# Another order of table, transpose and inverse steps for batch 0, the Gelu table ahead of the products, and batch 1 one slot later

## The chip, the cores and the metric

The kernel runs on one core of a Trainium2 chip. Its five engines work side by side, each through its own queue in program order: TensorE (PE in the profile) multiplies into PSUM, ScalarE (ACT) and VectorE (DVE) copy PSUM results to SBUF and compute on them, GpSimd (POOL) does small copies and issues loads, SyncE (SP) issues the other transfers. The metric is the device time of one execution in microseconds. Eight runs of the kernel before gave a median of 774.5 us (774.27 to 774.85).

## The reference

Every batch of `x` (8 x 3008 x 256) is filtered along the sequence in the frequency domain, and the result goes through a two-matrix block with an exact Gelu:

```python
X = np.fft.rfft(x, axis=1)
Y = X * (filt_r + 1j * filt_i)[None]
y = np.fft.irfft(Y, n=x.shape[1], axis=1)
h = y.reshape(B * S, D) @ w_in            # 24064 x 256 @ 256 x 2048
g = 0.5 * h * (1 + erf(h / sqrt(2)))
out = g @ w_out                           # 2048 -> 256
```

## The kernel before

The 3008-point transform is split as 47 x 64, so that each half is a matrix product with a small table of sines. Four tables are made on the chip: T1 for the 47-point half, T2 for the 64-point half with the twiddle factors in it (24 frequencies k, with three column blocks: sine-type rows in block 1, their swapped and signed twin in blocks 2 and 0), T3, which is T2's blocks 1 and 2 transposed, and T4 and T4c, T1 transposed with weights, for the inverse. `table_2_sin(h)` writes block 1 of one half of T2 on ScalarE, `table_2_swap(h)` makes the other blocks by two TensorE matmuls and, for h = 1, four ScalarE copies of 384 columns, `table_3(q)` transposes eight frequencies on TensorE and copies 1024 columns on ScalarE, `table_4` does the same for T4 and T4c.

**Batch 0** has no other work beside it, so it goes through SBUF and TensorE transposes and not through DRAM. Sixteen `c1` steps do the first half of the transform. `c1t(q)` transposes four frequencies (eight 128x128 transposes) and copies them to tile b(q). `c2(p)` does the second half for two frequencies: four matmuls into a two-bank PSUM tile, and one VectorE product of 1024 columns with the filter F, into tile p(p) (the last one, p = 11, in two pieces of 512). `c3(p)` takes products p and p + 1 through the inverse with T3: sixteen matmuls into two banks and two copies into `vt`; the matmuls of p + 1 stand in its second half. The two last products have a `c3` of eight matmuls each. After that come, in a loop of ten, `c3t` (transposes, a VectorE copy) and `c4` (matmuls with T4c, copies into the ring `y_sb`).

The transposes, `c3` and table steps share four PSUM banks (kind `n`) that are used in rotation, `c2` and the warm-up matmuls two tiles of two banks (kind `w`). A step that takes a bank waits until the copy of the tile four (or two) before it is done. The filter's lower half of partitions is copied to the upper half by `dup_filters`, two frequencies at a time: frequencies 0 to 3 on VectorE, the others on POOL, and product p needs the copy with its frequencies 2p and 2p + 1.

There is no scheduler: `manual_schedule` keeps every engine's instructions in the order in which the Python code issues them, and semaphores for the data and for the buffers are put in. So the order of the calls is the order of the work. In the loop `for q in range(7)` (L578) these calls stand.

**The main loop** (L648) runs over (47 + 1) x 16 slots, sixteen for each tile of 512 tokens. Slot s = 16 t + jc does a quarter of the output matmuls of tile t - 1 (`mm2`, L492) and one block of tile t's first matrix (`mm1`, L465) with its Gelu on ScalarE (L468). The transforms of batches 1 to 7 are put into chosen slots ahead of these by `put(slot, ...)`: `s1` (first half, four per batch, with SP writes to a DRAM tile R1), `r1` (four SP reads back), `s2` (twelve, with two ScalarE copies and three VectorE operations each), `s3` (four slots after its `s2`, SP writes to R2 for every two), `r2` (eight SP reads), `s4` (sixteen, into the ring), and `load_next`, POOL's loads of the next batch. For batch 1 the slots are: `s1` at 0, 4, 8, 12, `r1` at 15, `s2` from 25 on in steps of 2.8, `r2` at 61, `s4` from 68 on in steps of 0.72. Batch 1's rows begin in slot 80.

Of the kernel before, what the change touches and what calls it, by code (L numbers as in the profile page):

```python
# [9 lines left out]
AF = mybir.ActivationFunctionType  # L10
ALU = mybir.AluOpType
FP32 = mybir.dt.float32
BF16 = mybir.dt.bfloat16
# [4 lines left out]
NA, NB = 47, 64  # L18
K1 = 24
# [9 lines left out]
class _Mix:  # L29
# [187 lines left out]
        ts(out=self.wtc, in0=self.p, scalar1=4.0, scalar2=1.0, op0=ALU.is_ge, op1=ALU.add)  # L217


    def table_4(self):  # L220
        nc = self.nc
        ps = self.bank("ps_t4", "n")
        rows = ((self.T4, self.T1p, self.wt), (self.T4c, self.T1q, self.wtc))
        o = [ps[0:96, 128 * i:128 * i + 2 * NA] for i in range(2)]
        for i, (t4, t1, wt) in enumerate(rows):
            nc.tensor.matmul(o[i], lhsT=t1.rearrange("p a b c -> p (a b c)"),
                             rhs=self.eye[0:2 * NA, 0:2 * NA], start=True, stop=True)
        for i, (t4, t1, wt) in enumerate(rows):
            self._evac(t4.rearrange("p n h -> p h n"), o[i].rearrange("p (h n) -> p h n", h=2), "act", wt[0:96])

    def table_3(self, q, eng):
        ps = self.bank("ps_t3", "n", BF16)
# [277 lines left out]
@with_exitstack  # L510
def kernel(
    ctx: ExitStack,
    tc: tile.TileContext,
    x: bass.AP,
    filt_r: bass.AP,
    filt_i: bass.AP,
    moe_w_in: bass.AP,
    moe_w_out: bass.AP,
    out: bass.AP,
):  # L520
    m = _Mix(ctx, tc, x, filt_r, filt_i, moe_w_in, moe_w_out, out)
    nc, B, S = tc.nc, m.B, m.S
    NT = B * S // TCH
    ctx.enter_context(tc.manual_schedule())

    g = m.small
    wide = ctx.enter_context(ExitStack())
    m.psum(wide, w=(2, 2), n=(4, 1))
    act = "act"
    m.p = m.iota(g, "p", [128, 1], [[0, 1]], cm=1)  # L530
    m.load_x(0, 0, 1, (0,))
    m.pi = m.iota(g, "pi", [128, 1], [[0, 1]], cm=1, dt=I32)
    m.load_x(0, 0, 1, (1,))
    m.ones = g.tile([128, 512], BF16, name="ones")
    nc.vector.memset(m.ones, 1.0)
    m.warm_up(10)
    m.table_1(g)
    m.weights_4(g)
    m.T1c = g.tile([2 * NA, 96], BF16, name="T1c")
    nc.vector.tensor_copy(out=m.T1c.rearrange("p (k h r) -> p k h r", h=2, r=2),  # L540
                          in_=m.T1.rearrange("p (h r k) -> p k h r", h=2, r=2))
    m.kk = m.iota(g, "kk", [128, K1 // 2], [[1, K1 // 2]])
    m.jj = g.tile([128, NB], FP32, name="jj")
    for sgn, lo in ((1, 0), (-1, 32)):
        nc.gpsimd.iota(m.jj[:, lo:lo + 32], pattern=[[sgn * NA, 32]], base=min(0, sgn * NA),
                       channel_multiplier=0, allow_small_or_imprecise_dtypes=True)
    cols = m.iota(g, "cols", [128, 128], [[1, 128]])
    m.load_x(0, 1, 4)
    m.gen = m.py.tile([128, 3, K1 // 2, NB], FP32, tag="y", name="gen")
    m.table_2(g)  # L550
    m.table_2_angle(0)
    m.unit_matrices(g, cols)
    m.table_2_angle(1)
    for k, n in ((0, 4), (4, 4), (8, 8), (16, 8)):
        m.load_filters(k, n)
    m.dup_filters(nc.gpsimd, 4, 4)
    m.load_w_in()
    m.dup_filters(nc.gpsimd, 8, 8)


    warm = g.tile([128, 1], FP32, name="warm")
    for u in range(16):
        m.c1(u // 2, u % 2, act if u < 4 or u % 2 else False)
        if u == 3:
            m.warm_up(3)
            m.table_2_sin(0)
        if u == 7:
            m.table_2_swap(0)
            m.table_2_minus()
            m.warm_up(3)  # L570
        if u == 11:
            m.warm_up(2)
    m.table_2_sin(1)
    m.warm_up(2)
    m.c1t(0, False)
    m.c1t(1, act)
    m.dup_filters(nc.vector, 0, 4)
    for q in range(7):  # L578
        if q < 6:
            m.c2(2 * q)  # L580
            if q > 0 and q + 2 < 6:
                m.c1t(q + 2, act)
            m.c2(2 * q + 1)
        if q == 0:
            m.table_3(0, act)
            m.table_2_swap(1)
            m.dup_filters(nc.gpsimd, 16, 8)
            m.T1p = g.tile([2 * NA, 2, K1, 2], BF16, name="T1p")
            nc.gpsimd.tensor_copy(out=m.T1p, in_=m.T1.rearrange("p (h r k) -> p h k r", h=2, r=2))
            m.T1q = g.tile([2 * NA, K1, 2, 2], BF16, name="T1q")  # L590
            nc.gpsimd.tensor_copy(out=m.T1q, in_=m.T1.rearrange("p (h r k) -> p k r h", h=2, r=2))
            m.table_1_tiles(g)
            m.load_x(1)
            m.load_w_out(0)
            m.load_w_out(8)
            m.c1t(2, act)
        if 1 <= q < 3:
            m.table_3(q, act)
        if q >= 1:
            if q < 6:  # L600
                m.c3(2 * q - 2)
            else:
                m.table_4()
                m.c3(10, 1)
                m.c3(11, 1)
        if q == 4:

            nc.scalar.activation(out=warm, in_=m.p, func=AF.Gelu)
    wide.close()
    wide = ctx.enter_context(ExitStack())  # L610
    m.psum(wide, v=(5, 1), t=(3, 1))
    for u in range(10):
        if u < 8:
            m.c3t(u)
        if u >= 2:
            m.c4(u - 2, (act, False if u > 7 else act))
    wide.close()
    m.psum(ctx, h=(3, 1), o=(2, 1), f=(3, 1))


    at = {}

    def put(slot, f, *a):
        at.setdefault(slot, []).append((f, a))

    def first(b):
        return (b * S // TCH) * 16

    for b in range(1, B):
        hi = first(b)  # L630
        if b == 1:
            s1, n1, r1, s2, n2, r2, s4, n4 = 0, 4, 15, 25, 2.8, 61, 68, 0.72
        else:
            s1, n1, r1, s2, n2, r2, s4, n4 = hi - 94, 3.5, hi - 80, hi - 69, 3.5, hi - 24, hi - 17, 1
        for u in range(16):
            put(s4 + int(u * n4), m.s4, b, u // 2, u % 2)
        for c in range(4):
            put(s1 + int(c * n1), m.s1, b, c)
            put(r1, m.r1, b, c)
            put(r2, m.r2, b, c)  # L640
        for p in range(12):
            put(s2 + int(n2 * p), m.s2, b, p)
            put(s2 + int(n2 * p) + 4, m.s3, b, p)
        if b + 1 < B:
            for i in range(8):
                put(s2 + int(n2 * (i + 2)), m.load_next, b, i + 2, i // 2, i % 2)

    for s in range((NT + 1) * 16):  # L648
        t, jc = s // 16, s % 16
        for f, a in at.pop(s, ()):  # L650
            f(*a)
        if t >= 1:
            m.mm2(t - 1, jc)
        if t < NT:
            m.mm1(t, jc)
    assert not at
# [30 lines left out]
```

## Time and profile before

| | |
|---|---|
| median of 8 runs | 774.5 us (774.27 to 774.85) |
| profiled execution | 774.65 us, of which the span of the trace is 772.84 |
| TensorE busy | 757.2 us, 98% of the span |
| ScalarE, VectorE, POOL busy | 567.0, 397.7, 64.7 us |
| granted TensorE clock | 1.00 throughout |
| batch 0's products (first to last) | 16.89 to 32.34 us |
| last copy into `vt` | ends at 33.99 us |
| main loop's first TensorE instruction | 41.50 us |
| tile 0's `mm2` begins (slot 16) | 51.8 us |

Times inside the trace are microseconds from the start of the span. "Busy" counts computing instructions only. Instructions of an engine can overlap by about a tenth of a microsecond where they follow each other closely, so the cost of one in an unbroken run is read from start to start. A row of the timeline that stands for several instructions gives the start of the first and the time that they cover. A row's bracket names the idle time before it and what ended it; where an instruction waits for several things, the one that came last by the trace is named, and this can be one that had no part in it. Here that holds for the chain of waits, which leads into the main loop over a load of `x_sb` that landed at 42.0: the semaphore that the first `mm1` reads is shared by that load and by the load of `w_in`, which it needs and which had landed at 26.5.

### The profile page before, as it was taken

Reading aid. Unit: us, or ns where it says so; the run is one execution under the profiler, and the core shown is the slowest. Engines: PE = TensorE matmul, PEld = TensorE weight load, DVE = VectorE, ACT = ScalarE, POOL = GpSimd, SP = SyncE. Lnnn points to the kernel's source line nnn. Section 1 sums busy time; section 2 is a strip of 40 time slices with the busy share of each in tenths; the row PEclk is TensorE's granted clock in tenths of the full one; section 3 lists DMA queues with packets and bytes.
Section 4 is the critical chain, followed back from the end, with each engine's and each line's share of the span. In section 5 each row is a group of like instructions: output and inputs, shape, how many; then the busy total and the mean of one; then the engine's idle time right before and its main releaser. Section 6 shows DMA issues by size and latency. Waiting matters only on the chain.

```text
span 772.8 us, 14959 instructions
## 1 busy us (share of the span) xinstructions
PE 757.2 (98%) x5965; PEld 528.5 (68%) x6066; DVE 397.7 (51%) x722; ACT 567.0 (73%) x980; POOL 64.7 (8%) x161
## 2 busy tenths in 40 slices
PE   7899999999999999999999999999999999999998
PEld 4857775676776766676777676667776676766666
DVE  7866755464555645456463664636646366411011
ACT  5879955897568975689656996579865798666663
POOL 7801100020000100011000110001100000000000
PEclk9999999999999999999999999999999999999999
DMA  8895645466253661636516365254553422410111
GB/s 139 139 177 134 146 124 125 130 120 153 60 134 111 139 157 38 188 84 121 146 50 184 85 129 127 75 158 96 123 137 79 140 83 69 123 42 28 42 42 55
DMA packets 87398, 85.66 MB, mean 111 GB/s; under 512 B 6752, under 2 KB 77536, under 8 KB 87328
## 3 DMA queue, kind: packets, MB, share of 16 engines
q1 hardware_dynamic: 78816, 68.70, 31.1%
q0 software_dynamic: 8512, 16.00, 14.1%
q8 instruction: 47, 0.77, 0.4%
q14 instruction: 23, 0.19, 0.1%
HBM read 54.00 MB, written 46.66 MB: 130 GB/s over the span
## 4 chain that ended last, share of the span: by engine, by line
PE 94%; DMA 2%; POOL 2%; issue 1%; ACT 1%; DVE 0%; POOLq 0%
PE ps_o L492 43%; PE ps_h L465 39%; PE ps_s L324 3%; PE ps_s L349 3%; PE ps_s L299 2%; PE ps_s L276 2%; DMA x_sb<-in_x_dram 2%; POOL x_sb L82 1%; POOL F L96 1%; ACT T L249 0%; ACT b_sb L249 0%; PE ps_e L482 0%; ACT vt_sb L249 0%; PE ps_c L387 0%; DVE at_sb L251 0%
## 5 line engine op out<-in xcount | busy, mean ns | idle before, releaser
L468 ACT ACTIVATE g_sb<-ps_h 128x512 bf16<-128x512 f32 x752 | 437.9, 597 | 182.9 <-PE ps_h L465 154.6
L492 PE MATMUL ps_o<-w_out_sb,g_sb 128*128 128x256 bf16 x2992 | 447.6, 273 | 2.1
L465 PE MATMUL ps_h<-y_sb,w_in_sb 128*128 128x512 bf16 (+3 forms) x1500 | 424.3, 366 | 0.2 <-DMA x_sb<-in_x_dram 0.2
L492 PEld LDWEIGHTS <-g_sb 128*128 128x128 bf16 x2992 | 283.8, 98 | 134.5 <-issue 9.9
L465 PEld LDWEIGHTS <-w_in_sb 128*128 128x128 bf16 x1600 | 154.7, 98 | 23.2 <-issue 0.8
L498 DVE COPY ost<-ps_o 128x512 f32<-128x512 f32 x93 | 63.9, 687 | 144.3 <-PE ps_o L492 144.2
L307 DVE TENSOR_TENSOR p<-ps_s,F 128x512 bf16<-128x512 f32 x84 | 58.1, 692 | 105.2 <-ACT p L306 89.1
L253 DVE TENSOR_SCALAR y_sb<-ps_s 128x376 bf16<-128x376 f32 x112 | 61.0, 548 | 80.5 <-PE ps_s L349 80.5
L251 DVE CAST a_sb<-ps_s 128x512 bf16<-128x512 f32 x112 | 69.4, 683 | 27.1 <-PE ps_s L276 27.1
L251 DVE CAST v_sb<-ps_s 128x512 bf16<-128x512 f32 x84 | 57.4, 685 | 2.9 <-PE ps_s L324 2.8
L305 ACT ACTIVATE p<-ps_s 64x512 bf16<-64x512 f32 x84 | 49.8, 593 | 2.0
L306 ACT CAST p<-ps_s 64x512 bf16<-64x512 f32 x84 | 48.5, 577 | 1.0
L349 PEld LDWEIGHTS <-d_sb 96*128 96x128 bf16 x448 | 30.8, 97 | 25.3
L101 POOL COPY gate<-p 1x1 bf16<-1x1 bf16 x48 | 8.5, 176 | 470.5 <-DVE p L309 470.5
L349 PE MATMUL ps_s<-T,d_sb 96*128 96x94 bf16 x448 | 36.3, 204 | 1.1
L309 DVE TENSOR_TENSOR p<-p 128x512 bf16<-128x512 bf16 x84 | 35.7, 425 | 2.9
L308 DVE TENSOR_TENSOR p<-p,F 128x512 bf16<-128x512 bf16 x84 | 34.9, 416 | 0.0
L324 PE MATMUL ps_s<-p,T 128*128 128x256 bf16 x168 | 32.1, 273 | 2.0
L82 POOL DMA_DIRECT2D x_sb<-in_x_dram x64 | 32.5, 510 | 13.3 <-issue 12.9
L299 PE MATMUL ps_s<-b_sb,T 128*128 128x256 bf16 x168 | 32.1, 273 | 0.0
L324 PEld LDWEIGHTS <-T 128*128 128x128 bf16 x168 | 16.4, 98 | 19.8 <-DVE p L309 0.4
L299 PEld LDWEIGHTS <-T 128*128 128x128 bf16 x168 | 16.4, 98 | 13.4
(103 smaller groups left out, 189.3 us busy)
## 6 DMA issues: line engine op xcount, KB each, us to landing
out_dram<-ost SPq DMA_DIRECT2D x93, 256.0 KB, 2.3
x_sb<-in_x_dram POOLq DMA_DIRECT2D x64, 188.0 KB, 3.6
R<-a_sb SPq DMA_DIRECT2D x112, 96.0 KB, 2.1
b_sb<-R SPq DMA_DIRECT2D x28, 384.0 KB, 4.3
R<-v_sb SPq DMA_DIRECT2D x42, 256.0 KB, 3.3
d_sb<-R SPq DMA_DIRECT2D x56, 192.0 KB, 4.6
w_in_sb<-in_moe_w_in_dram POOLq DMA_DIRECT2D x2, 512.0 KB, 7.2
w_out_sb<-in_moe_w_out_dram POOLq DMA_DIRECT2D x2, 512.0 KB, 11.8
```

What stands on the lines that cost most here:

```text
L251: self.nc.vector.tensor_copy(out=out, in_=in_)
L253: self.nc.vector.tensor_scalar(out=out, in0=in_, scalar1=scale, scalar2=None, op0=ALU.mult)
L299: nc.tensor.matmul(ps[:, 256 * i:256 * i + 256], lhsT=self.T2[:, k, 1:3].rearrange("p a b -> p (a b)"), rhs=self.st[b, "b", k // 6][:, k % ...
L305: nc.scalar.activation(out=p2[0:64], in_=ps[64:128], func=AF.Copy, scale=-1.0)
L306: nc.scalar.copy(out=p2[64:128], in_=ps[0:64])
L307: nc.vector.tensor_tensor(out=p1, in0=ps, in1=f(0), op=ALU.mult)
L324: nc.tensor.matmul(ps[:, 256 * i:256 * i + 256], lhsT=self.T3[:, k].rearrange("p a b -> p (a b)"), rhs=w[:, 256 * i:256 * i + 256], start= ...
L349: nc.tensor.matmul(ps[:, 94 * i:94 * i + 94], lhsT=d[:, (grp % 2) * 4 + i, 128 * half:128 * half + 128], rhs=t4, start=True, stop=True)
L465: nc.tensor.matmul(ps[:, o:o + n], lhsT=self.w_in_sb[:, dc, jc * 128:jc * 128 + 128], rhs=self.ring[:, dc, off:off + n], start=(dc == 0), ...
L468: nc.scalar.activation(out=self.st["g", t][:, jc, :], in_=ps, func=AF.Gelu)
L492: nc.tensor.matmul(ps[:, tile_i % 2, :], lhsT=g[:, jc, tile_i * 128:tile_i * 128 + 128], rhs=self.w_out_sb[:, jc, :], start=(jc == 0), sto ...
L498: nc.vector.tensor_copy(out=ost, in_=ps)
```

## The change

`table_4` makes one of its two tables per call. T4c, which batch 0 needs, is made before c2(9), T4 in slot 20 of the main loop. The second sine of T2 is issued right after c1's eighth step instead of after all sixteen. The Gelu table is loaded ahead of `c1t(0)`; before, it was loaded between c3(6) and c2(10). The loop over q is written out in a new order: T3(0) ahead of c2(0), c1t(2) between c2(0) and c2(1), c1t(3) after c3(0), the swap of T2's second half after c2(3) instead of after T3(0), c3 interleaved with c2 two by two, `c1t(5)`'s copy on VectorE instead of ScalarE, c2(11) after c3(8). On POOL T1q comes ahead of the last four filter copies. Batch 1's `s1`, `r1`, `s2` and with it `s3` and `load_next` are one slot later; `r2` and `s4` stay.

```diff
-    def table_4(self):
-        nc = self.nc
-        ps = self.bank("ps_t4", "n")
-        rows = ((self.T4, self.T1p, self.wt), (self.T4c, self.T1q, self.wtc))
-        o = [ps[0:96, 128 * i:128 * i + 2 * NA] for i in range(2)]
-        for i, (t4, t1, wt) in enumerate(rows):
-            nc.tensor.matmul(o[i], lhsT=t1.rearrange("p a b c -> p (a b c)"),
-                             rhs=self.eye[0:2 * NA, 0:2 * NA], start=True, stop=True)
-        for i, (t4, t1, wt) in enumerate(rows):
-            self._evac(t4.rearrange("p n h -> p h n"), o[i].rearrange("p (h n) -> p h n", h=2), "act", wt[0:96])
+    def table_4(self, t4, t1, wt, tag="n"):
+        ps = self.bank("ps_t4", tag)
+        self.nc.tensor.matmul(ps[0:96, 0:2 * NA], lhsT=t1.rearrange("p a b c -> p (a b c)"),
+                              rhs=self.eye[0:2 * NA, 0:2 * NA], start=True, stop=True)
+        self._evac(t4.rearrange("p n h -> p h n"), ps[0:96, 0:2 * NA].rearrange("p (h n) -> p h n", h=2), "act",
+                   wt[0:96])
...
             m.warm_up(3)
+            m.table_2_sin(1)
         if u == 11:
             m.warm_up(2)
-    m.table_2_sin(1)
+
+    nc.scalar.activation(out=warm, in_=m.p, func=AF.Gelu)
     m.warm_up(2)
     m.c1t(0, False)
     m.c1t(1, act)
     m.dup_filters(nc.vector, 0, 4)
-    for q in range(7):
-        if q < 6:
-            m.c2(2 * q)
-            if q > 0 and q + 2 < 6:
-                m.c1t(q + 2, act)
-            m.c2(2 * q + 1)
-        if q == 0:
-            m.table_3(0, act)
-            m.table_2_swap(1)
-            m.dup_filters(nc.gpsimd, 16, 8)
-            m.T1p = g.tile([2 * NA, 2, K1, 2], BF16, name="T1p")
-            nc.gpsimd.tensor_copy(out=m.T1p, in_=m.T1.rearrange("p (h r k) -> p h k r", h=2, r=2))
-            m.T1q = g.tile([2 * NA, K1, 2, 2], BF16, name="T1q")
-            nc.gpsimd.tensor_copy(out=m.T1q, in_=m.T1.rearrange("p (h r k) -> p k r h", h=2, r=2))
-            m.table_1_tiles(g)
-            m.load_x(1)
-            m.load_w_out(0)
-            m.load_w_out(8)
-            m.c1t(2, act)
-        if 1 <= q < 3:
-            m.table_3(q, act)
-        if q >= 1:
-            if q < 6:
-                m.c3(2 * q - 2)
-            else:
-                m.table_4()
-                m.c3(10, 1)
-                m.c3(11, 1)
-        if q == 4:
-
-            nc.scalar.activation(out=warm, in_=m.p, func=AF.Gelu)
+    m.T1q = g.tile([2 * NA, K1, 2, 2], BF16, name="T1q")
+    nc.gpsimd.tensor_copy(out=m.T1q, in_=m.T1.rearrange("p (h r k) -> p k r h", h=2, r=2))
+    m.dup_filters(nc.gpsimd, 16, 8)
+    m.T1p = g.tile([2 * NA, 2, K1, 2], BF16, name="T1p")
+    nc.gpsimd.tensor_copy(out=m.T1p, in_=m.T1.rearrange("p (h r k) -> p h k r", h=2, r=2))
+    m.table_1_tiles(g)
+    m.load_x(1)
+    m.load_w_out(0)
+    m.load_w_out(8)
+    m.table_3(0, act)
+    m.c2(0)
+    m.c1t(2, act)
+    m.c2(1)
+    m.c2(2)
+    m.c3(0)
+    m.c1t(3, act)
+    m.c2(3)
+    m.table_2_swap(1)
+    m.c2(4)
+    m.table_3(1, act)
+    m.c3(2)
+    m.c2(5)
+    m.c1t(4, act)
+    m.c2(6)
+    m.c3(4)
+    m.table_3(2, act)
+    m.c2(7)
+    m.c1t(5, False)
+    m.c2(8)
+    m.c3(6)
+    m.table_4(m.T4c, m.T1q, m.wtc)
+    m.c2(9)
+    m.c2(10)
+    m.c3(8)
+    m.c2(11)
+    m.c3(10, 1)
+    m.c3(11, 1)
...
         if b == 1:
-            s1, n1, r1, s2, n2, r2, s4, n4 = 0, 4, 15, 25, 2.8, 61, 68, 0.72
+            s1, n1, r1, s2, n2, r2, s4, n4 = 1, 4, 16, 26, 2.8, 61, 68, 0.72
...
+    put(20, m.table_4, m.T4, m.T1p, m.wt, "f")
     for s in range((NT + 1) * 16):
```

## The prediction

> **What bounds the kernel now.** I read the page's busy lines first:
>
> ```profile
> PE 757.2 (98%) x5965; PEld 528.5 (68%) x6066; DVE 397.7 (51%) x722; ACT 567.0 (73%) x980; POOL 64.7 (8%) x161
> ...
> PE   7899999999999999999999999999999999999998
> ```
>
> TensorE (PE) is busy in nine tenths or more of every slice but the first two and the last. So from about 42 us on, when the main loop starts, time is TensorE's own work, and only two things can move the end: when the main loop starts, and whether a wait opens inside it. The change works on the first slices, so the view of busy time by stretches comes next (columns: stretch and length, busy PE, PE weight loads, DVE, ACT, POOL, granted clock, DMA share, GB/s); the first five rows are batch 0's products, then its inverse steps, then main-loop slots 0 to 15:
>
> ```profile
> 14.70:17.60 2.90, 2.55 (x34) 2.27 (x34) 2.16 (x4) 1.73 (x2) 2.90 (x6) 1.00 1.07 143
> 17.60:21.20 3.60, 3.07 (x39) 2.60 (x38) 3.49 (x4) 3.56 (x7) 3.56 (x6) 1.00 1.09 152
> 21.20:24.30 3.10, 3.10 (x46) 2.90 (x46) 2.23 (x3) 3.10 (x5) 3.10 (x5) 1.00 1.09 168
> 24.30:29.10 4.80, 4.62 (x66) 4.20 (x64) 4.50 (x5) 4.39 (x8) 4.80 (x6) 1.00 0.73 146
> 29.10:34.00 4.90, 3.52 (x45) 2.80 (x43) 3.66 (x5) 4.74 (x11) 4.73 (x14) 1.00 0.51 84
> 34.00:41.50 7.50, 6.71 (x128) 6.32 (x128) 6.31 (x10) 5.48 (x14) 2.44 (x4) 1.00 1.05 174
> 41.50:51.80 10.30, 10.07 (x63) 3.77 (x66) 9.50 (x16) 7.30 (x15) 0.00 (x0) 1.00 1.04 185
> ```
>
> In the product stretches no engine is the single bound: VectorE (DVE), ScalarE (ACT), GpSimd (POOL) and TensorE take turns, so the order decides. The granted clock is 1.00 throughout. The timeline (start, length, engine, line, what, count) says who waits:
>
> ```profile
> 18.55 1.64 ACT L249 ACTIVATE T<-ps_sw 128x384 bf16<-128x384 f32 x4
> ...
> 21.35 7.91 POOL L96 COPY F<-F 64x1024 bf16<-64x1024 bf16 x8
> ...
> 21.84 1.10 ACT L249 ACTIVATE T<-ps_t 128x1024 bf16<-128x1024 bf16 x1
> ...
> 22.52 2.51 DVE L392 TENSOR_TENSOR p<-ps_c,F 128x1024 bf16<-128x1024 f32 x2 [0.81 <-PE ps_c L387]
> ...
> 22.71 0.60 PE L387 MATMUL ps_c<-b_sb,T 128*128 128x256 bf16 x4
> 22.75 1.18 ACT L249 ACTIVATE vt_sb<-ps_c 128x512 bf16<-128x512 f32 x2
> ...
> 23.70 1.14 ACT L249 ACTIVATE b_sb<-ps_c1t 128x1024 bf16<-128x1024 bf16 x1
> ...
> 25.33 5.81 DVE L392 TENSOR_TENSOR p<-ps_c,F 128x1024 bf16<-128x1024 f32 x5 [0.30 <-POOL F L96]
> ...
> 30.15 1.28 ACT L608 ACT_TABLE_LOAD   x1
> ...
> 31.06 1.28 DVE L396 TENSOR_TENSOR p<-ps_c,F 128x512 bf16<-128x512 f32 x2
> ...
> 31.55 1.06 ACT L249 ACTIVATE vt_sb<-ps_c 128x512 bf16<-128x512 f32 x2
> ...
> 32.51 0.36 ACT L249 ACTIVATE T<-ps_t,wt 96x94 bf16<-96x94 f32 x1
> ...
> 33.56 0.42 DVE L251 CAST vt_sb<-ps_c 128x256 bf16<-128x256 f32 x1 [1.22 <-PE ps_c L409]
> ...
> 34.04 1.50 PE L428 MATMUL ps_c3t<-eye,vt_sb 128*128 128x128 bf16 x24 [0.52 <-DVE vt_sb L251]
> ```
>
> Twelve products p0 to p11 of L392/L396 are the spine: 25.33 to 32.34 is one unbroken run on VectorE, broken before it twice (0.81 us at p4, 0.30 at p6, whose first operand comes from the TensorE step just before it, so the POOL named there is not the cause). ScalarE is unbroken from 17.64 to about 28.6, and its Gelu table load falls at 30.15. The last product ends at 32.34, the last vt copy at 33.99 (33.56 + 0.42), and 34.04 starts the inverse transposes. From there 7.5 us of work, untouched by the change, lead to 41.50.
>
> **Prices, from these rows and their neighbours in the same view** (start to start where a run is unbroken). ScalarE: a 1024-wide copy 0.91 (21.84 to 22.75), one vt copy 0.48 (22.75 to 23.70 for two), a swap copy 0.37 (18.55 to 20.04 for four). VectorE: a product 1.14 in a run (25.33 to 31.06 for five), 1.23 after a wait. TensorE: eight transposes 0.45 (22.26 to 22.71), one c2 0.44, one c3 0.89 (28.18 to 29.07). From a c2's start to its product 0.69 (24.64 to 25.33). From a c3's start to its first vt copy 0.87 (28.18 to 29.05). POOL's filter copies 0.98 each (21.35, eight of them). I laid the old order out with these prices, each engine in its own order, each step after its operand and after its PSUM bank comes free (four banks in rotation for transposes and c3, two pairs for c2): p6 ends at 26.52, p11 at 32.30, the last vt copy at 33.92, where the profile has 26.56, 32.34 and 33.99. So the walk is good to 0.1 us on most steps; at p5 it is 0.18 early.
>
> **Part 1: sine of the second table half moved up (table_2_sin(1), 0.84 us).** It leaves 14.56 and goes in behind the swap copies that end at 10.90, with its angle ready at 10.93. ScalarE idles 0.82 us there, until 11.72, so it costs nothing; without that cover it would delay one 0.49 us copy.
>
> **Part 2: table load ahead of the products.** In the row it takes 1.28, the dummy Gelu after it adds 0.11 net. Moved, it runs from 14.68 (the last copy of step 1) to 16.19. Cost there: b(1)'s copy ends at 17.10 instead of 16.84, 0.26 later, and c2(2), its reader, waits anyway until p0 frees a bank at 17.99. Gain: ScalarE's tail loses 1.40 us at 30.15.
> The Trainium skill, ScalarE: Activation LUTs, What ACT_TABLE_LOAD costs, puts a switch at 1.28 us plus a drain of 1.38, some 2.66 in all. The row has the first part alone: the copy before ends at 30.13, the load starts at 30.15, the next instruction at 31.44. By the page b(1) would come at about 18.5 and the sum below would grow by some 0.7 us; I go by the row.
>
> **Part 3: the new order, walked.** TensorE: T3(0)'s transposes fill the wait for b(0); c2(0) 16.10, c1t(2) 16.54, c2(1) 16.98, c2(2) 18.04. ScalarE: T3(0) done 18.02, b(2) 18.93, earlier than before by 0.6 and 2.2. Then c3(0) starts at 18.48, but its second half needs p1, which VectorE ends at 19.12: TensorE is held until then and leaves c3(0) at 19.61. Behind it in TensorE's queue stand c1t(3), c2(3), the two swap matmuls and c2(4), done 21.27; ScalarE idles 0.6 us for the first of them. ScalarE then has: two vt copies to 20.66, b(3) 21.57, swap copies 21.96, 22.34, 22.73, 23.11. In the old order the swaps were done by 20.19. VectorE meanwhile: p0 to p4 end at 17.99, 19.12, 20.63, 21.95, 23.72 (before: 18.12, 19.25, 20.58, 21.71, 23.74); p2 and p4 hang on POOL's copies (19.32 and 22.42), which stay put.
> Now the new wait. T3(1)'s second half reads the swapped table, so TensorE holds it for the third swap copy at 22.73; c3(2) follows at 23.00 and only then c2(5), at 23.89, where the old order had it at 22.71. Product p5 ends at 25.78 (before 25.03): VectorE idle 0.83. Next c3(4)'s second half waits for p5, T3(2) stands behind it, c2(7) starts at 26.72, p7 ends at 28.61 (before 27.69), 0.47 idle. Then c1t(5)'s copy, moved from ScalarE to VectorE, adds 0.61: 29.22. From there products are unbroken: 30.35, 31.49, 32.62, halves 33.33 and 33.93, which is 1.6 us after the old 32.34. The tail is shorter, since table load and table-4 copies are gone from it: c3(11) follows at once, last vt copy 34.82, 0.89 after the last product instead of 1.65. Walk against walk: 34.82 - 33.92 = **+0.90 us**. Bounds: if T3(1) must wait for all four swap copies, +0.38; if p5 starts as p4 ends, the run is p5 24.85, p6 25.99, p7 27.12, copy 27.73, p11 32.33, vt 33.22, that is -0.70. The third copy is what the old trace shows: T3(1) started at 19.73 and issued its eight unbroken (0.61 to the end of the last), so its fifth went at 19.96, before the fourth swap copy ended at 20.19.
>
> **Part 4: POOL and the transfers.** T1q (0.28) goes ahead of the last four filter copies; the first of them is needed by p8 at 29.22 and comes at 26.6. Sum up to load_x(1) unchanged, so its eight loads still start at 30.44; the first two land at 33.8 and 34.9, needed after 42. Filters, w_in, w_out: same place in the queue. Nothing.
>
> **Part 5: T4 from the tail into slot 20.** One matmul of 94 columns (0.05 start to start, 0.21 to its end) and a 0.36 copy on ScalarE, where slots 16 to 25 have slack on it (7.04 of 10 busy from 50 to 60). +0.05, bounds 0 and 0.21. Its reader s4 is 48 slots off.
>
> **Part 6: batch 1 one slot later.** Moved: s1 (32 matmuls, 16 VectorE casts, 16 SP transfers), r1 (4 transfers), s2 and s3 with 6 SP writes, 8 gates and x loads on POOL. Slots 0 to 15: TensorE does the same sixteen mm1 and four s1; the two waits of 0.39 and 0.36 us for VectorE's casts come from the four-slot spacing, which stays; r1 and s2 keep their distance. Zero. But r2 and s4 do not move: between the last s3 (slot 60, was 59) and s4 (slot 68) one slot of 0.87 is lost. In the old trace the last v_sb write is issued at 95.78, both d_sb halves of the first quarter have landed by 101.59, s4's weight load is at 101.97: 0.38 to spare. The ost copy stands ahead of p11's chain on VectorE in the new order instead of between it and the v casts, so I get that write only 0.35 later: just covered. +0.05, bounds 0 and 0.49.
>
> **Sum.** 0.90 + 0.05 + 0.05 = +1.0 us. The profiled execution took 774.65 (span 772.84 and 1.81 around it), 0.15 over the median 774.5; on it 775.65, against the median **775.5**, +0.13%. What a measurement here can tell from no change is about 0.2%, 1.55 us.
>
> **Rivals.** *Slower beyond 0.2%: T3(1) is let go later.* The fourth swap copy (+0.38), and p5 starting 0.15 to 0.2 late as the walk was in the old order: 774.5 + 0.90 + 0.38 + 0.18 + 0.10 = 776.1, and 776.2 if p7 is late alike. It decides from a p5 start of 25.15 on (walk: 24.55). For it: ScalarE, TensorE and VectorE are chained here with no slack. Against: the old trace's release after the third copy.
> *Faster: no starvation at p5.* c2(5) is out by 23.0, the run stays whole, -0.70 + 0.05: 773.9. For it: the tail's 1.4 us on ScalarE is really freed. Against: c2(5) would have to come 0.9 us sooner, past two transposes' worth of queue and the swap copies.
> *Late d_sb:* s4 held by up to 0.49: 776.0. Against: the 0.38 to spare.
> *Clock:* new TensorE holes (0.6 at 17.4, 1.3 at 21.3) drop the clock; the opening warm-ups run at 0.43 each against 0.21 later, so 2 to 3 us of the stage would double: 778. Against: the old trace has TensorE busy 3.52 of 4.90 us from 29.1 to 34, with holes of 0.3 to 0.5, at clock 1.00.
>
> **How the numbers follow.** Forecast 0.42 (its own range 774.9 to 776.0), later T3(1) 0.40, no starvation 0.09, late d_sb 0.06, clock 0.03. Faster by over 0.2% (below 772.95) needs a full microsecond more than the second rival gives: 0.04. Slower by over 0.2% (above 776.05) is three quarters of the first rival, half of late d_sb, and the clock: 0.36. The rest is 0.60. Range: from the second rival, 773.9, to the first with the upper bounds of T4 and s4, 774.5 + 1.46 + 0.21 + 0.49 = 776.7.
>
> **What would show it.** Right: p5 starts near 24.5 after an idle of 0.8 with c2(5) as releaser; last vt copy near 34.8; mm1 starts near 42.4; no ScalarE gap at 30; s4 at slot 68 waits under 0.1. Wrong: p4 to p11 unbroken with the main loop before 41.5, or s4 waiting on d_sb, or a clock under 1.00 before 42.

## The result and the profile after: 776.9 us, slower by 0.31%

The changed kernel took 776.88 us (median of 11 runs, 776.33 to 777.27), the kernel before beside it 774.46 (31 runs, 773.96 to 775.73). The ratio is 1.0031 (95% interval 1.0023 to 1.0038): 2.42 us more, where the forecast was 1.0 and the range ended at 776.7. The direction and the place were right, the size was not. Beyond 0.2% was given a chance of 0.36.

The profiled execution took 776.82 us (span 775.0), 2.17 more than that of before. The page of the changed kernel, engines and slices:

```profile
PE 756.9 (98%) x5965; PEld 527.5 (68%) x6066; DVE 398.5 (51%) x723; ACT 566.7 (73%) x979; POOL 64.7 (8%) x161
...
PE   7899999999999999999999999999999999999998
```

TensorE's busy time is the same (757.2 before), so the 2.2 us are idle time. They are too little to be seen in slices of 19 us; the view of busy time by stretches finds them (stretch and length, PE, weight loads, DVE, ACT, POOL, clock, DMA share, GB/s). The first four stretches are those shown of before; the last three are the rest of batch 0's products, its inverse steps, and slots 0 to 15:

```profile
14.70:17.60 2.90, 2.61 (x39) 2.25 (x36) 2.46 (x4) 2.89 (x4) 2.90 (x7) 1.00 1.12 145
17.60:21.20 3.60, 3.24 (x40) 2.81 (x41) 3.16 (x4) 2.79 (x5) 3.56 (x6) 1.00 1.10 148
21.20:24.30 3.10, 1.95 (x31) 1.73 (x30) 1.88 (x2) 3.00 (x7) 3.10 (x4) 1.00 1.07 180
24.30:29.10 4.80, 4.30 (x62) 3.83 (x61) 3.69 (x4) 3.71 (x6) 4.68 (x6) 1.00 0.71 137
29.10:35.30 6.20, 4.57 (x53) 3.41 (x54) 5.60 (x7) 3.46 (x8) 6.04 (x14) 1.00 0.62 99
35.30:42.70 7.40, 6.71 (x128) 6.30 (x127) 6.28 (x10) 5.48 (x14) 1.09 (x3) 1.00 1.14 189
42.70:53.00 10.30, 9.93 (x61) 3.61 (x64) 8.88 (x16) 7.26 (x14) 0.00 (x0) 1.00 0.83 149
```

From 21.20 to 24.30 TensorE is busy 1.95 us of 3.10 (3.10 before) and VectorE 1.88 (2.23 before), while ScalarE is full. The timeline (start, length, engine, line, what, count, idle time before and what ended it) shows what stands there:

```profile
19.45 1.09 ACT L245 ACTIVATE vt_sb<-ps_c 128x512 bf16<-128x512 f32 x2 [0.81 <-PE ps_c L405]
...
20.42 1.03 ACT L245 ACTIVATE b_sb<-ps_c1t 128x1024 bf16<-128x1024 bf16 x1
...
21.33 1.66 ACT L245 ACTIVATE T<-ps_sw 128x384 bf16<-128x384 f32 x4
22.16 1.23 DVE L388 TENSOR_TENSOR p<-ps_c,F 128x1024 bf16<-128x1024 f32 x1 [0.31 <-POOL F L96]
22.66 0.23 PEld L230 LDWEIGHTS <-T 128*128 128x128 bf16 x4 [1.32 <-ACT T L245]
22.66 0.40 PE L230 MATMUL ps_t<-eye,T 128*128 128x128 bf16 x4 [1.15 <-ACT T L245]
...
23.79 0.60 PE L383 MATMUL ps_c<-b_sb,T 128*128 128x256 bf16 x4
...
24.89 2.36 DVE L388 TENSOR_TENSOR p<-ps_c,F 128x1024 bf16<-128x1024 f32 x2 [1.50 <-PE ps_c1t L371]
...
27.77 1.23 DVE L388 TENSOR_TENSOR p<-ps_c,F 128x1024 bf16<-128x1024 f32 x1 [0.52 <-POOL F L96]
...
33.06 1.29 DVE L392 TENSOR_TENSOR p<-ps_c,F 128x512 bf16<-128x512 f32 x2
...
34.84 0.42 DVE L247 CAST vt_sb<-ps_c 128x256 bf16<-128x256 f32 x1 [0.49 <-PE ps_c L405]
```

The four swap copies stand on ScalarE behind c3(0)'s two copies (19.45) and b(3) (20.42). T3(1)'s second half waits 1.15 us for the third of them, which ends at 22.61 by the trace (the fourth ends at 22.99, after the transposes have gone on at 22.66). c2(5) stands behind it (23.79), and VectorE is idle 1.50 before p5 and 0.52 before p7. Two of the names in brackets are not the cause: p5 and p7 wait for the c2 ahead of them (23.79 and 27.07), and the POOL copy that p7 needs had ended at 25.05. The last vt copy ends at 35.26 (33.99 before) and the last y_sb copy at 42.72 (41.45).

The loads of x that end step 1 happened to land 0.29 us earlier in this execution. So I count batch 0 from the end of VectorE's last at_sb copy (ScalarE's ends 0.02 to 0.14 us later) to the end of the last y_sb copy ("the stage"): 14.66 to 41.45 = 26.79 us before, 14.37 to 42.72 = 28.35 after, **+1.56**. Main loop, from there to the start of the last Gelu: 721.47 before, 722.40 after, **+0.93**. 1.56 + 0.93 - 0.29 = 2.20, against 2.17 between the two profiled executions. TensorE's waits of the changed kernel (for what, us in total, times, longest) name two of the main loop's parts:

```profile
PE ps_s L345 <- DMA d_sb<-R: 0.3, 1, 0.3
...
PE ps_s L320 <- DVE p L305: 0.2, 1, 0.2
```

Compared Gelu by Gelu with the trace of before, the main loop loses 0.19 us in slots 0 to 15, 0.04 where T4 now stands, 0.15 at the last s3 (slot 60), 0.28 at the first s4 (slot 68), and 0.27 at batch 3's s4 near 288 us.

### The profile page after: what moved, and what is told of

Read it like the earlier page. It is cut to its first block, busy times and chain, and to the rows that moved or that the text cites. A ratio compares the mean times of both kernels' runs of the same rounds, so it can differ in the third digit from the quotient of the medians.

```text
span 775.0 us, 14957 instructions
## 1 busy us (share of the span) xinstructions
PE 756.9 (98%) x5965; PEld 527.5 (68%) x6066; DVE 398.5 (51%) x723; ACT 566.7 (73%) x979; POOL 64.7 (8%) x161
## 4 chain that ended last, share of the span: by engine, by line
PE 92%; POOL 3%; DMA 2%; issue 1%; ACT 1%; DVE 0%; SPq 0%; POOLq 0%
PE ps_o L488 43%; PE ps_h L461 39%; PE ps_s L320 3%; PE ps_s L345 3%; PE ps_s L295 2%; PE ps_s L272 2%; POOL F L96 1%; DMA w_out_sb<-in_moe_w_out_dram 1%; POOL x_sb L82 1%; DMA x_sb<-in_x_dram 1%; POOL F L91 1%; DMA d_sb<-R 0%; PE ps_e L478 0%; ACT g_sb L464 0%; ACT p L301 0%
```

## The experiments

All times are medians, ratios are to the kernel before on the same chip. "Loop" is the main loop's length in the profiled execution less that of before, split as above. All runs together, in us:

| run | ratio (95%) | stage | loop | slots 0-15 | s3 | first s4 | later batches |
|---|---|---|---|---|---|---|---|
| before | 1 | 26.79 | 0 | 0 | 0 | 0 | 0 |
| changed | 1.0031 (1.0023 to 1.0038) | 28.35 | +0.93 | 0.19 | 0.15 | 0.28 | 0.27 |
| x1_old_slots | 1.0026 (1.0016 to 1.0036) | 28.36 | +0.66 | 0 | 0 | 0.33 | 0.28 |
| x2_swap_early | 1.0015 (1.0006 to 1.0024) | 27.08 | +1.04 | 0.18 | 0.15 | 0.29 | 0.37 |
| x3_vectore_pad | 1.0032 (1.0020 to 1.0045) | 27.95 | +0.77 | 0.17 | 0.14 | 0.40 | 0 |
| x4_before_new_slots | 1.0010 (1.0001 to 1.0019) | 26.79 | +0.51 | 0.18 | 0.15 | 0.19 | 0 |
| y1_swap_pad_slots_act | 0.9995 (0.9981 to 1.0010) | 26.89 | +0.05 | 0 | 0 | 0 | 0 |
| y2_gelu_late | 1.0032 (1.0018 to 1.0045) | 28.37 | +1.13 | 0.17 | 0.15 | 0.59 | 0.17 |
| y3_before_gelu_early | 0.9990 (0.9980 to 1.0000) | 26.40 | +0.46 | 0 | 0 | 0 | 0.42 |
| y4_before_again | one run, 774.19 us | 26.84 | 0.00 | 0 | 0 | 0 | 0 |
| z1_searched_order | 0.9995 (0.9984 to 1.0006) | 25.89 | +0.04 | 0 | 0 | 0 | 0 |
| z2_scalare_pad | one run, 776.38 us | 28.37 | +0.86 | 0.18 | 0.14 | 0.49 | 0 |
| z3_s4_one_later | 1.0033 (1.0017 to 1.0050) | not compared | +0.59 | 0.18 | 0.15 | 0 | 0.21 |

The split leaves out some 0.04 us for T4 where it is moved. The stage repeats within 0.05 us for the same order (26.79, 26.84 and 26.79; 28.35, 28.36, 28.37 and 28.37), so it is a sharper measure of an order than the medians.

A second profile of the kernel before, unchanged, was taken for this table:

> The kernel before once more, for a second profile. Theory A (the 0.38 us between the landing of the first d_sb quarter and its first reader is a margin that transfer times eat in some executions): the landing moves by 0.2 to 0.6 us against the first profile's. Rival B (it is steady): within 0.1 us. 774.2 to 774.8.

It differs from the first by 0.05 us in the stage and by 0.01 in the loop. The margin at the first s4 was 0.25 us in place of 0.38, which lies between the two theories.

### The swap after c2(2) instead of after c2(3)

```diff
     m.c2(2)
+    m.table_2_swap(1)
     m.c3(0)
     m.c1t(3, act)
     m.c2(3)
-    m.table_2_swap(1)
     m.c2(4)
```

> The changed kernel with table_2_swap(1) issued between c2(2) and c3(0) instead of after c2(3). Theory A (T3(1) is held for the swap copies, which stand on ScalarE behind c3(0)'s two copies and b(3); this starves VectorE at p5): p5 ends 1.0 to 1.1 us earlier, the last vt copy 1.0 to 1.1 us earlier, 775.8. Rival B (the engines are so full between 18 and 25 us that the four swap copies only push c3(0)'s copies and b(3) back, and T3(1) waits for PSUM banks instead): p5 within 0.3 us of the changed kernel's, 776.6 to 776.9.

The stage fell by 1.27 us to 27.08, the time to 775.29 (ratio 1.0015). Timeline of this run, TensorE and VectorE:

```profile
20.56 0.61 PE L230 MATMUL ps_t<-eye,T 128*128 128x128 bf16 x8
...
23.22 2.35 DVE L388 TENSOR_TENSOR p<-ps_c,F 128x1024 bf16<-128x1024 f32 x2 [0.20 <-PE ps_c1t L371]
```

T3(1) now runs its eight transposes without a break at 20.56, and p5 starts at 23.22 after 0.20 us of idle. So 1.27 of the stage's 1.56 us were that wait, more than the 1.0 to 1.1 expected; the moved copy of c1t(5), the table load and POOL's order are still as in the changed kernel.

### One instruction more on VectorE

p5 starts 0.449 us after its wait is over by the trace's record of that wait, in the kernel before 0.447. p4 and p6 take 0.045 and 0.044 in the kernel before. Both p5s are the 64th instruction of VectorE, counted with its wait instructions. So:

```diff
     m.warm_up(2)
+    nc.vector.memset(g.tile([128, 1], FP32, name="pad"), 0.0)
     m.c1t(0, False)
```

> The changed kernel with one 128x1 memset on VectorE, in its idle time ahead of c1t(0)'s copy, so that every later VectorE instruction stands one place further back in its queue. In both profiles p5 starts 0.45 us after the wait ahead of it is over, where every other product that waited starts after 0.04; p5 is the 64th VectorE instruction in both. Theory P (the lag belongs to the place in the queue): p5 starts 0.04 after its wait, 0.40 earlier, the last vt copy 0.4 earlier, 776.45. Rival D (the lag belongs to p5's own operands: its filter copy, its PSUM pair): p5 still 0.45 late, 776.85.

p5's lag fell from 0.449 to 0.043 us, and the stage by 0.40 to 27.95. The timeline of the run with the pad:

```profile
24.33 2.36 DVE L388 TENSOR_TENSOR p<-ps_c,F 128x1024 bf16<-128x1024 f32 x2 [1.00 <-PE ps_c L383]
```

The idle time before p5 is 1.00 where it was 1.50. A memset that computes nothing made batch 0 shorter, so the place in the queue is the cause, not p5's operands. The total does not settle it: the ratio is 1.0032, the median of the five runs 1.86 us above the kernel before beside it (the changed kernel's was 2.42 above), and 0.4 us is less than the interval of the ratio. In the profiled execution the first s4 waited 0.40 instead of 0.28.

### One instruction more on ScalarE

The main loop's first Gelu is ScalarE's 64th instruction in the changed kernel and starts 0.352 us after its wait; in the kernel before it is the 67th, at 0.046.

```diff
+    nc.scalar.activation(out=warm, in_=m.p, func=AF.Gelu)
     nc.scalar.activation(out=warm, in_=m.p, func=AF.Gelu)
```

> The changed kernel with the small Gelu ahead of the products issued twice, so that one more instruction stands in ScalarE's queue; nothing else. In the changed kernel's profile the main loop's first Gelu is ScalarE's 64th instruction and starts 0.35 us after its wait is over, where the kernel before has it 67th at 0.05. Place in the queue (theory P): the first Gelu starts under 0.06 after its wait, and the instruction that is now the 64th, ScalarE's last y_sb copy, starts some 0.35 after its own wait; the stage's end moves by 0 to +0.3. What the Gelu is or waits for (rival): its 0.35 stays. Either way the main loop's start-up loss of 0.19 us stays if it comes from the s1 step that now stands in slot 1 (776.8 in all, 776.6 to 777.2); it goes if it came from the late first Gelu (776.5).

The first Gelu's lag fell to 0.042. The last y_sb copy showed no lag, but by the trace it became the 63rd instruction and not, as I expected, the 64th; the 64th is now the wait instruction ahead of the Gelu. So the run shows that the lag leaves the Gelu with its place, and not where it would go. The Gelu itself came 0.31 us sooner after the stage, but by slot 16 the loop was late by 0.18 as before. The kernel has three PSUM tiles for mm1, which would cover a late first Gelu; that is argued, not shown. The loss in slots 0 to 15 comes with the slots alone, as the next pair shows.

### Batch 1's slots alone

Old slots in the changed kernel, and new slots in the kernel before:

```diff
-            s1, n1, r1, s2, n2, r2, s4, n4 = 1, 4, 16, 26, 2.8, 61, 68, 0.72
+            s1, n1, r1, s2, n2, r2, s4, n4 = 0, 4, 15, 25, 2.8, 61, 68, 0.72
```

> The changed kernel with batch 1's slots as before (s1 at 0, r1 at 15, s2 from 25); all of batch 0's new order stays, and T4 stays in slot 20. Theory A (the shift by one slot opens waits in the main loop: s3(11) on p11's chain 0.15 us, s4(0) on d_sb 0.28 us): 776.3 to 776.5, no wait of TensorE on d_sb at slot 68, and the lag behind the kernel before, 1.5 us at tile 0's end, grows by T4's 0.04 alone until slot 80. Rival B (the shift is covered, as the prediction had it, and the whole loss is batch 0's): 776.8 to 776.9, and the wait on d_sb stays.

```diff
-            s1, n1, r1, s2, n2, r2, s4, n4 = 0, 4, 15, 25, 2.8, 61, 68, 0.72
+            s1, n1, r1, s2, n2, r2, s4, n4 = 1, 4, 16, 26, 2.8, 61, 68, 0.72
```

> The kernel before with only batch 1 one slot later (s1 at 1, r1 at 16, s2 from 26). Theory A (the shift opens waits at s3(11) and s4(0), 0.15 and 0.28 us, and 0.1 to 0.2 at the start of the main loop): 774.9 to 775.1. Rival B (covered): 774.5.

The shift costs time in either kernel. The 0.17 to 0.19 us in slots 0 to 15 and the 0.14 to 0.15 at s3 stand in all seven profiles with the new slots and in none of the others. In the kernel before the shift added 0.51 us in the profile, and over the runs it has the ratio 1.0010 (1.0001 to 1.0019); in the changed kernel, undoing it took the ratio from 1.0031 to 1.0026, where the intervals overlap. One thing in the changed kernel with old slots went against my expectation: it still waited 0.33 us for d_sb at the first s4.

The wait at s3 is one step that the timeline shows. VectorE of the kernel before (p11's three operations end with the row at 93.53), and its first s4 on TensorE:

```profile
93.53 0.42 DVE L309 TENSOR_TENSOR p<-p 128x512 bf16<-128x512 bf16 x1
93.87 0.68 DVE L498 COPY ost<-ps_o 128x512 f32<-128x512 f32 x1
94.47 1.28 DVE L251 CAST v_sb<-ps_s 128x512 bf16<-128x512 f32 x2
...
102.18 0.50 PE L349 MATMUL ps_s<-T,d_sb 96*128 96x94 bf16 x8
```

VectorE of the changed kernel (p11's three operations end with the row at 96.17), then TensorE:

```profile
94.53 0.68 DVE L494 COPY ost<-ps_o 128x512 f32<-128x512 f32 x1
95.13 0.68 DVE L303 TENSOR_TENSOR p<-ps_s,F 128x512 bf16<-128x512 f32 x1
95.72 0.42 DVE L304 TENSOR_TENSOR p<-p,F 128x512 bf16<-128x512 bf16 x1
96.17 0.42 DVE L305 TENSOR_TENSOR p<-p 128x512 bf16<-128x512 bf16 x1
96.52 1.28 DVE L247 CAST v_sb<-ps_s 128x512 bf16<-128x512 f32 x2
```

```profile
96.66 0.39 PE L320 MATMUL ps_s<-p,T 128*128 128x256 bf16 x2 [0.19 <-DVE p L305]
...
104.11 0.51 PE L345 MATMUL ps_s<-T,d_sb 96*128 96x94 bf16 x8 [0.33 <-DMA d_sb<-R]
```

The output copy ost, 0.6 us, now stands ahead of p11's chain (before: behind it, 93.87 after 93.53), so s3 waits for p11, and the last v_sb copies end at 97.80 instead of 95.75: 2.05 later, where the loop as a whole is 1.50 late here. That is 0.55 less for the transfers, of which s4 gets back 0.15 by the wait at s3. The spare time before was 0.38, so 0.40 less would be just about covered. The transfers make the rest: in this execution the last v_sb write took 2.42 us from issue to landing in place of 2.27, and the first two d_sb reads 3.68 in place of 3.41. That is 0.44 too late; 0.28 of it shows, as the weight load stood 0.21 us ahead of its matmul before (101.97 and 102.18).

### The first s4 one slot later as well

```diff
-            s1, n1, r1, s2, n2, r2, s4, n4 = 1, 4, 16, 26, 2.8, 61, 68, 0.72
+            s1, n1, r1, s2, n2, r2, s4, n4 = 1, 4, 16, 26, 2.8, 61, 69, 0.72
```

> The changed kernel with batch 1's s4 one slot later as well (69 for 68), so that its distance to the last s3 is that of the kernel before. Theory A (s4 waited for d_sb because it came a slot nearer to the writes): no wait at the first s4, 0.2 to 0.4 us less, 776.4 to 776.7, main loop +0.5 to +0.7 against the kernel before where the changed one had +0.93. Theory B (the transfers of batch 1 themselves take longer in this arrangement, or their time varies by a few tenths of a us from run to run, and the slot has no part in it): a wait of 0.2 us or more at the first s4 stays, 776.8 to 777.1.

The wait for d_sb at the first s4 was gone, and the loop was +0.59 as the first theory had it; the other parts stayed. The ratio did not fall (1.0033, median 776.72, which is 2.15 above the kernel before beside it in place of 2.42): its interval is wider than the 0.3 us in question. The profiled execution had a low TensorE clock between 5 and 25 us (below), so only its loop is compared.

The first s4 waited for d_sb in all six profiles that have the new slots and s4 at 68 (0.19 to 0.59), in one of six that have the old slots, and not here. So the lost slot is what took the margin. It is not the whole cause: in the six profiles with the wait the first two reads took 3.64 to 3.79 us, against 3.41 in the first profile of the kernel before, and the write 2.27 to 2.66. Nor were the old slots safe: in the five of them where TensorE did not wait, the reads had landed 0.04 to 0.38 us before the weight load. For the exception the view of the transfers has a row to show: 94 to 105 us, what, queue, count, KB each, median us from issue to landing. First the changed kernel with old slots, which waited, then the one with all losses undone (below), which has old slots and did not:

```profile
R<-v_sb SPq DMA_DIRECT2D x1, 256.0 KB, 2.6
```

```profile
R<-v_sb SPq DMA_DIRECT2D x1, 256.0 KB, 2.3
```

The last write took 2.6 us in place of 2.3, which is most of a margin of 0.38 (0.25 in the second profile of the kernel before); the first two reads took 3.98 and 3.82. What makes a transfer slower in one execution is not shown.

### The Gelu table

Back to its old place, behind c3(6), in the changed kernel; and early, with the sine early and T4 in slot 20, in the kernel before:

```diff
-    nc.scalar.activation(out=warm, in_=m.p, func=AF.Gelu)
     m.warm_up(2)
...
     m.c3(6)
+    nc.scalar.activation(out=warm, in_=m.p, func=AF.Gelu)
```

> The changed kernel with the Gelu table loaded after c3(6), where it was before, and not ahead of the products. Theory A (in the changed order products on VectorE set the end and ScalarE has holes of 0.9 and 1.5 us around 29 and 31 us, which take the load of 1.4): last vt copy at the same distance from the last at_sb copy within 0.1 us, 776.8 to 776.9. Rival B (the shorter tail of the changed order comes from the early load): 1.4 us later, 778.2. Rival C (the early load delays b(1) and T3(0) and is part of the loss): 0.2 to 0.3 earlier, 776.6.

```diff
...
+            m.table_2_sin(1)
...
-    m.table_2_sin(1)
+    nc.scalar.activation(out=warm, in_=m.p, func=AF.Gelu)
...
-                m.table_4()
+                m.table_4(m.T4c, m.T1q, m.wtc)
...
-        if q == 4:
-            nc.scalar.activation(out=warm, in_=m.p, func=AF.Gelu)
...
+    put(20, m.table_4, m.T4, m.T1p, m.wt, "f")
```

> The kernel before, with three parts of the change alone: second sine up, Gelu table ahead of the products, T4 in slot 20 (so that c3(10) comes after T4c alone); the order of the product steps and batch 1's slots as before. Theory A (in the old order ScalarE's tail, table load and two table-4 copies stand between the last products and the last vt copies): last vt copy 0.3 to 0.4 us earlier, 774.0 to 774.2. Rival B (VectorE's last product and its c3 set that end alone): no change, 774.4 to 774.6.

In the new order the place of the table load makes no difference (28.37 against 28.35): at its old place (30.20 to 31.48 in that run) it lies in the idle time that ScalarE has in the changed kernel around 31 us. In the old order the three moves together gain 0.39 us of the stage, all of it behind the last product: from that product's end to the last vt copy it is 1.26 us in place of 1.65, so the old tail has ScalarE on its path. 773.89 us is the fastest of all, but its interval reaches 1.0000, and a wait of 0.42 us for another batch's d_sb stood in the execution that was profiled.

### All losses undone, and another order

The edits of the swap, the pad and the old slots above, together in the changed kernel, and c1t(5)'s copy back on ScalarE:

```diff
-    m.c1t(5, False)
+    m.c1t(5, act)
```

> The changed kernel with four edits: table_2_swap(1) between c2(2) and c3(0), one memset ahead on VectorE so that p5 is no longer its 64th instruction, c1t(5)'s copy back on ScalarE, batch 1's slots as before. Theory A (these four are where the changed kernel loses): from the last at_sb copy to the last y_sb copy 26.3 to 26.5 us, against 28.35 in the changed kernel and 26.79 in the one before; time 774.0 to 774.4. Rival B (ScalarE is as full as VectorE between 18 and 30 us, so c1t(5) there pushes T3(2) and c3's copies back, and p8 waits): 26.9 to 27.2 us, 774.7 to 775.0.

774.22 us, ratio 0.9995, stage 26.89, loop +0.05: the changed kernel's whole loss is back, and nothing of what I expected beyond that. Its 26.89 is the number of rival B, but not its mechanism: p8 follows p7 without a wait. Late are p2 and p4 (19.25 and 22.56). Each starts 0.03 us after the POOL filter copy that it needs (ended 19.22 and 22.53); counted from the start of the stage these ended 0.3 and 0.5 us later than in the changed kernel, as POOL waited for loads of F in this execution (0.28 and 0.24 us). What the stage would be without that is not shown.

The last try was an order found by walking many orders with this document's prices. It starts from the kernel before with the three moves (sine and Gelu table early, T4 in slot 20) and the pad:

```diff
+    m.table_3(0, act)
     m.c1t(1, act)
     m.dup_filters(nc.vector, 0, 4)
-    for q in range(7):
...
+    m.c2(0)
+    m.table_2_swap(1)
...
+    m.c1t(2, act)
+    m.c2(1)
+    m.c1t(3, act)
+    m.c2(2)
+    m.c2(3)
+    m.c1t(4, act)
+    m.c3(0)
+    m.c2(4)
+    m.c1t(5, act)
+    m.c2(5)
+    m.table_3(1, act)
+    m.c3(2)
+    m.c2(6)
+    m.c2(7)
+    m.c3(4)
+    m.c2(8)
+    m.table_3(2, act)
+    m.c2(9)
+    m.c3(6)
+    m.table_4(m.T4c, m.T1q, m.wtc)
+    m.c2(10)
+    m.c2(11)
+    m.c3(8)
+    m.c3(10, 1)
+    m.c3(11, 1)
```

> Taken from the kernel before with the sine early, the Gelu table ahead of the products and T4 in slot 20, batch 1 in its old slots. New here: another order of batch 0, found by walking many orders with the prices of the profile: the swap of T2's second half after c2(0), table copies of c1t(1) to c1t(5) all on ScalarE and each one or two products ahead of use, c3(0) after c1t(4), T3(1) after c2(5), T3(2) after c2(8); and one 128x1 memset on VectorE, so that p5 is not the 64th VectorE instruction. Theory A (what bounds batch 0 is which step stands ahead of which in the three queues, and the walk prices it): last vt copy 0.8 us earlier than in the run with only the three moves, stage from last at_sb copy to last y_sb copy 25.4 to 25.8 us (26.40 there, 26.8 before), 773.0 to 773.4 in all. Theory B (each new order has its own small losses of 0.1 to 0.3 us at a step, as the changed kernel had, and the walk sees them too late): stage 26.2 to 26.6, 773.7 to 774.3. If the swap copies or c1t(3), c1t(4) come late on ScalarE, p6 or p8 shows an idle VectorE.

The stage came to 25.89 us: 0.90 below before, 0.51 below the three moves alone, where the walk said 0.8. p10 starts 0.32 late behind T4c (T4c's transposed operand comes late from POOL), which the walk had not. The time is 774.51 us, ratio 0.9995 (0.9984 to 1.0006), so the 0.9 us of the stage did not show in the total, though the interval would still hold it. In the profiled execution the clock was 0.69 between 10 and 15 us and step 1 ended 0.7 us later than in the kernel before; but the executions at clock 1.00 took as long (774.09 to 774.99), so where the gain went in them is open. No kernel here is shown to be faster than the one before.

## Why the prediction missed

Point by point, by its own steps. The changed profile starts 0.29 us earlier than the walk, which is taken off the walk's times here.

- **What bounds batch 0: right.** The order of three queues decides it. Moving one pair of matmuls and their four copies three calls up was worth 1.27 us.
- **Part 1 (sine early) and Part 4 (POOL): right.** Neither shows a wait.
- **Part 2 (table load): right in size, its worth was not asked.** Load and dummy Gelu took from 14.40 to the next copy at 15.81, 1.41 us, so the row's 1.4 held. The 2.66 us of the Trainium skill, ScalarE: Activation LUTs, What ACT_TABLE_LOAD costs, is not what this place shows. The 1.40 us taken off ScalarE's tail was worth, together with the moves of the sine and of T4, 0.39 in the old order; by itself it was worth nothing in the new.
- **Part 3 (the walk): right chain, wrong size. This is the first step that failed: +0.90 was +1.56.** T3(1) went on after the third swap copy, as walked, at 22.66 (walk 22.44); c2(5) came at 23.79 (23.60). 0.40 of the missing 0.66 is p5's lag as the 64th instruction. I had seen it in the old order, as the walk being "0.18 early at p5", and carried it only into a rival; but it stood there at 0.45 behind cover, and the new order took the cover away. Another 0.22 is the price of the third swap copy. The walk gave each copy its time from start to start (0.37 to 0.39) and let T3(1) go on after that, but T3(1) waits for the copy's end. The copy started at 22.07, where the walk had it within 0.02, and ended at 22.61, 0.54 later, where the walk had 22.44; from there to the transpose it is 0.05. In the old order nothing waited for such an end: the third copy had ended at 19.81 and the fifth transpose went at 19.96. The walk also had p1's end 0.13 early, but c3(0)'s first copy behind it came only 0.04 late (19.45 for 19.41).
- **Part 5 (T4): right**, 0.04 for 0.05.
- **Part 6 (one slot later): the second step that failed: +0.05 was 0.62 in the changed profile (0.19, 0.15 and 0.28), without batch 3's wait of 0.27.** "Zero" for slots 0 to 15 was 0.18 in seven profiles. What in these sixteen slots loses it is not settled; half is at their start, where TensorE's first instruction, now an mm1 in place of an s1, comes 0.15 us after the last y_sb copy (42.87 after 42.72) in place of 0.06 (41.51 after 41.45). I had noted that the ost copy would stand ahead of p11's chain, and used it for the write's time alone, not for s3, which reads p11. And "just covered" was a margin of 0.38 from one execution, in which the transfers were at their shortest: in the changed profile they took 0.42 longer.
- **Rivals.** *T3(1) let go later* was the nearest in time (776.1) and for the wrong reason in its larger part: the fourth copy was not waited for. Its smaller part, the late p5, is what came; its turning point, p5 at 25.15, was just passed (24.89 + 0.29 = 25.18). *Late d_sb* came as well, with 0.19 to 0.59, so two rivals held together, which only the upper end of the range had added up. *No starvation* and the *clock* were wrong for the changed kernel's profile.
- **Left open:** waits of 0.17 to 0.42 us at d_sb of a later batch (the last column), in six of thirteen profiles, two of them with the old slots. They come and go between kernels that do not touch those batches; I have no cause that a run shows. The margin there is thin: in the first profile of the kernel before, batch 3's reads landed 0.18 us before the first weight load that needs them.
- **The sum:** 1.56 + 0.04 + 0.62 + 0.27 = 2.49 us by the profiles, where the medians differ by 2.42 and the forecast was 1.0.

## What to carry to other kernels

A step that a walk has 0.1 or 0.2 us early is a cost that is covered, not an error to drop: look at the lag itself, from the end of the wait to the start, before the order around it is changed. The time from start to start is the price of a step for what stands behind it in the same queue; whoever waits for its result waits for its end (0.37 and 0.54 us for a swap copy here). When an order of several queues is changed, write down for each queue what stands behind a wait, and ask for each new wait whether its operand can be made one place sooner. A distance in slots between writes and reads is a margin to be set against the spread of the transfers over several profiles, not against one.

## What the runs showed of the hardware that was not expected

- **The 64th instruction of VectorE and of ScalarE, directly behind a wait, starts late.** VectorE's 64th instruction, counted with the waits, started 0.44 to 0.46 us after its wait in the eight profiles where the 64th is p5 directly behind its wait. Batch 0's other products directly behind a wait started after 0.043 to 0.046. With one instruction inserted ahead the 64th is the wait itself, and the lag was gone. On ScalarE it was 0.352 or 0.353 us for the first Gelu where that was the 64th, and 0.042 to 0.046 where it was the 65th to 67th. It is not every 64th: VectorE's 768th, directly behind a wait in four profiles, started after 0.044 or 0.045. The runs show the place, not what happens there.
- **The clock in the opening differs between executions.** Windows of one execution, that of the run with s4 at 69, and then of the changed kernel:

```profile
5.00:10.00 5.00, 2.66 (x26) 1.20 (x24) 4.72 (x14) 2.48 (x5) 3.12 (x7) 0.94 1.03 175
10.00:15.00 5.00, 4.84 (x37) 3.13 (x35) 3.29 (x6) 3.29 (x7) 3.34 (x7) 0.50 0.98 152
15.00:20.00 5.00, 4.95 (x60) 3.88 (x58) 3.27 (x6) 3.97 (x7) 4.96 (x9) 0.88 1.08 143
```

```profile
5.00:10.00 5.00, 2.90 (x38) 1.82 (x37) 4.72 (x14) 3.24 (x7) 3.52 (x7) 1.00 0.98 169
10.00:15.00 5.00, 4.04 (x50) 2.54 (x51) 4.08 (x8) 4.05 (x8) 3.42 (x7) 1.00 1.09 174
```

The granted clock (third number from the right) fell to 0.50 in one and stayed at 1.00 in the other, in the same work; TensorE was busy 2.66 and 2.90 us of the five before. The execution with the low clock took 781.69 us in place of 776.7. Kernels of either order had such executions (one of the kernel before took 777.78 us at a mean clock of 0.993), so the rival on the clock was about something real, but not about the change.
